# Half feature tiles as pairs of 64-row score matmuls, one projection ahead of the scores, and a last store issued before its waits, in a diffusion transformer block

## The chip, the cores and the metric

The kernel runs on one core of one Trainium2 chip. The metric is device time in microseconds (us) for one execution. Three plain runs of the kernel before are given, and one further execution taken with the hardware profiler. "Faster" and "slower" below are against the median of the plain runs.

## The reference

One block of a diffusion transformer, in bfloat16, for 2 batch rows of 256 tokens (512 tokens together) with 1152 features, 2 heads of 576 features and a hidden layer of 4608.

```python
B, N, D = x.shape            # 2, 256, 1152
H = 2
Dh = D // H                  # 576
mod = (_silu(c) @ w_mod).reshape(B, 6, 1, D)
shift_a, scale_a, gate_a, shift_m, scale_m, gate_m = [mod[:, i] for i in range(6)]
h = _layernorm(x, axis=-1) * (1 + scale_a) + shift_a
qkv = (h @ wqkv).reshape(B, N, 3, H, Dh)
q, k, v = (qkv[:, :, 0].copy(), qkv[:, :, 1].copy(), qkv[:, :, 2].copy())
attn = _softmax(jnp.einsum('bqhd,bkhd->bhqk', q, k) * Dh ** (-0.5), axis=-1)
a = jnp.einsum('bhqk,bkhd->bqhd', attn, v).reshape(B, N, D) @ wo
x = x + gate_a * a
h2 = _layernorm(x, axis=-1) * (1 + scale_m) + shift_m
m = _gelu(h2 @ w_fc1) @ w_fc2
return x + gate_m * m
```

## The kernel before

The 1152 features are nine tiles of 128, so a head of 576 features is four and a half tiles. Feature tiles stand on the 128 partitions, tokens along the free axis. `QK` holds 18 tiles of 512 tokens: Q tiles 0 to 8 and K tiles 9 to 17. Head 0 has Q tiles 0 to 3 and the lower half (partitions 0 to 63) of tile 4; head 1 has the upper half of tile 4 and tiles 5 to 8. K tile 13 is shared by the heads in the same way.

The program is first recorded as units (a unit is one instruction on most engines, or a group of matmuls on TensorE) with the regions of memory that they read and write, and from these `Sched` derives which must wait for which. TensorE (PE) and the queue of SyncE (SP) run in the order in which the code writes them. VectorE (DVE), ScalarE (ACT) and GpSimd (POOL) have a written order for their first instructions (`S.first`) and after that the order of a small cost model: of the units that are ready, the one with the longest path behind it. `emit` then writes the engines' streams, with semaphore waits ahead of the instructions that need them.

The stages on PE, in the order written:

1. Modulation, layer norm transposes and the K projection, paced by the first weights to land.
2. The Q projection of tiles 0 to 5, one feature tile of the input at a time, into six PSUM banks (`qb`). Then `qk_evac` copies each bank to `QK`, on ACT and DVE in turn (`ev_rr`). Tile 4 is an exception: ACT copies its lower half to `QK[0:64, 4]`, whose upper half a memset (`z4a`, in `S.first` of DVE) has set to zero, and DVE copies its upper half to `Q4B`, whose lower half is zero. So each head has its own 128-row form of the shared tile, with zeros in the other head's rows.
3. Q tiles 6, 7 and 8 (`proj`, nine matmuls of 512 columns each) and the scores, in turns. `s_and_softmax(b, h)` computes the scores of one batch row and head in one bank (`s_bank`): for each of two query tiles (`jq`) five accumulating matmuls of 256 columns (`head_chunks`; -1 stands for `Q4B`), so 40 in all. Behind each block DVE finds the row maxima (L934) and scales them, ACT takes the exponential (L938), and DVE normalises (L942).
4. The V projection (`v_proj`), with the transposes of the four probability blocks (`pt_transposes`) between its pieces, and `rows`, which computes the remaining modulation rows with four column-tiled matmuls side by side (`quad_mm`).
5. Attention times V (`pv`), the output projection (`wo_tile`) with the second layer norm, fc1 with GELU, and fc2.

The output leaves in fc2: for each of four token tiles pieces of the 1152 features, in the last tile of widths 384, 384, 224, 96 and 64. Of each piece DVE multiplies by the gate (L1145) and adds the residual (L1146), and SP stores it. These are 14 stores. In `run_engine` SP waits, ahead of the last store, for the landing of all stores but the last two:

```python
if ins is last_out:
    for o in outs[:-2]:
        eng_handle.wait_ge(dma_sems[o.dma_sem], o.dma_val)
```

and after it for the last two. All DMA issues are recorded at L662, all ordinary matmuls at L681, the copies out of PSUM at L676 (ACT) and L678 (DVE).

Of the kernel before, what the change touches and what calls it, by code (L numbers as in the profile page):

```python
# [171 lines left out]
class Sched:  # L172
# [225 lines left out]
    def emit(self, nc, block, sems, dma_sems):  # L398
        order = self.order
        eidx = {e: 0 for e in ENGINES}  # L400
        dma_cnt = [0] * len(dma_sems)
        n_other = getattr(self, "n_other_dma_sems", 8)
        n_sp = len(dma_sems) - n_other
        di = 0
        dj = 0
        for e in ENGINES:
            for u in order[e]:
                for ins in u.instrs:
                    if u.dma_bytes > 0:
                        if e == "sp":  # L410
                            k = di % n_sp
                            di += 1
                        else:
                            k = n_sp + dj % n_other
                            dj += 1
                        dma_cnt[k] += 16
                        ins.dma_sem = k
                        ins.dma_val = dma_cnt[k]
                    else:
                        eidx[e] += 1  # L420
                        ins.eidx = eidx[e]
        self.final_counts = dict(eidx)
        self.final_dma = list(dma_cnt)
        snap = {}
        stats = {"waits": 0}

        def sem_of(d):
            if d.dma_sem is not None:
                return ("d", d.dma_sem), d.dma_val
            return ("e", d.unit.eng), d.eidx  # L430

        allu = sorted(self.units, key=lambda u: (u.start, u.uid))
        known = {e: {} for e in ENGINES}
        waits = {}
        for u in allu:
            e = u.eng
            kn = known[e]
            for ins in u.instrs:
                need = {}
                for d in ins.deps:  # L440
                    k, v = sem_of(d)
                    if need.get(k, 0) < v:
                        need[k] = v
                wl = []
                for k, v in sorted(need.items(), key=lambda kv: (-kv[1], str(kv[0]))):
                    if kn.get(k, 0) >= v:
                        continue
                    wl.append((k, v))
                    kn[k] = v
                    for d in ins.deps:  # L450
                        if sem_of(d) == (k, v):
                            sn = snap.get(d.gidx)
                            if sn:
                                for kk, vv in sn.items():
                                    if kn.get(kk, 0) < vv:
                                        kn[kk] = vv
                            break
                waits[ins.gidx] = wl
                stats["waits"] += len(wl)
                snap[ins.gidx] = dict(kn)  # L460
        self.wait_stats = stats

        outs = [ins for u in order["sp"] for ins in u.instrs if ins.is_out]
        last_out = outs[-1]

        def run_engine(e, eng_handle):
            for u in order[e]:
                for ins in u.instrs:
                    if ins is last_out:
                        for o in outs[:-2]:  # L470
                            eng_handle.wait_ge(dma_sems[o.dma_sem], o.dma_val)
                    for (k, v) in waits[ins.gidx]:
                        if k[0] == "d":
                            eng_handle.wait_ge(dma_sems[k[1]], v)
                        else:
                            eng_handle.wait_ge(sems[k[1]], v)
                    bi = ins.fn(eng_handle)
                    if ins.dma_sem is not None:
                        bi.then_inc(dma_sems[ins.dma_sem], 16)
                    else:  # L480
                        bi.then_inc(sems[e], 1)
            if e == "sp":
                for o in outs[-2:-1]:
                    eng_handle.wait_ge(dma_sems[o.dma_sem], o.dma_val)
                eng_handle.wait_ge(dma_sems[last_out.dma_sem], last_out.dma_val)

        block.sync(lambda eng: run_engine("sp", eng))
        block.tensor(lambda eng: run_engine("pe", eng))
        block.scalar(lambda eng: run_engine("act", eng))
        block.vector(lambda eng: run_engine("dve", eng))  # L490
        block.gpsimd(lambda eng: run_engine("pool", eng))
# [25 lines left out]
def c_mm(n):  # L517
    return max(n / 2.4 + 2.5, 27.0)
# [26 lines left out]
def build_kernel(nc, x, c, wqkv, wo, w_mod, w_fc1, w_fc2, out):  # L545
    S = Sched()
# [4 lines left out]
    with (  # L551
# [11 lines left out]
        def ps32(bank, c0=0, n=512):  # L563
            return psum[:, bank * 512 + c0: bank * 512 + c0 + n]
# [100 lines left out]
        def dve(cost, fn, reads, writes, name):  # L665
            return S.op("dve", cost, fn, reads=reads, writes=writes, name=name)
# [192 lines left out]
                k_pair((KT - 2, KT - 1), i, b)  # L859

        def qk_evac(j, bank):
            if j == 4:
                for eng, dst, src in (("act", QK[0:64, 4, :], psum[0:64, bank * 512:bank * 512 + 512]),
                                      ("dve", Q4B[64:128, :], psum[64:128, bank * 512:bank * 512 + 512])):
                    copy_on(eng, dst, src, 512, False, "qk_ev4" + eng)
                return
            copy_on("act" if ev_rr[0] % 2 == 0 else "dve", QK[:, j, :], ps32(bank), 512, False, "qk_ev%d" % j)
            ev_rr[0] += 1

        def proj(W, j, dst_j, H, bank):  # L870
# [1 line left out]
            for kt in range(KT):  # L872
                mm(ps32(bank), W[:, kt, j * 128:(j + 1) * 128], H[:, kt, :], kt == 0, kt == KT - 1)
            qk_evac(dst_j, bank)

        dve(330, lambda e: e.memset(QK[64:128, 4, :], 0.0), [], [QK[64:128, 4, :]], "z4a")

        def quads(w, g0, g1, q):
            return w.rearrange("p (g q c) -> p g q c", q=4, c=32)[:, g0:g1, q, :]
# [16 lines left out]
        for kt in range(KT):  # L896
            for b in range(2):
# [5 lines left out]
                else:  # L903
# [6 lines left out]
        S.first = {  # L910
# [5 lines left out]
        }  # L916


        head_chunks = {0: [(0, 9), (1, 10), (2, 11), (3, 12), (4, 13)], 1: [(-1, 13), (5, 14), (6, 15), (7, 16), (8, 17)]}
        s_bank = {(0, 0): 4, (1, 0): 5, (0, 1): 6, (1, 1): 3}  # L920

        def s_and_softmax(b, h):
            idx = b * 2 + h
            bank = s_bank[(b, h)]
            S.unit("pe", 10 * c_mm(256), "S_%d_%d" % (b, h))
            ch = head_chunks[h]
            for jq in range(2):
                for ci, (gq, gk) in enumerate(ch):
                    q0 = b * 256 + jq * 128
                    l = Q4B[:, q0:q0 + 128] if gq < 0 else QK[:, gq, q0:q0 + 128]  # L930
                    mm(ps32(bank, jq * 256, 256), l, QK[:, gk, b * 256:(b + 1) * 256], ci == 0, ci == len(ch) - 1)
            s3 = ps32(bank).rearrange("p (j k) -> p j k", j=2)
            mx, nb, rsum, ri, pp = MX[:, idx, :], NB[:, idx, :], RS[:, idx, :], RI[:, idx, :], PP[idx]
            dve(c_dve_psum32(512), lambda e: e.tensor_reduce(out=mx, in_=s3, axis=AX.X, op=ALU.max), [s3], [mx], "smax_%d" % idx)  # L934
            dve(165, lambda e: e.tensor_scalar(out=nb, in0=mx, scalar1=-SCALE, scalar2=None, op0=ALU.mult), [mx], [nb], "snb_%d" % idx)
            for jq in range(2):
                o, i_, bb, aa = pp[:, jq, :], ps32(bank, jq * 256, 256), nb[:, jq:jq + 1], rsum[:, jq:jq + 1]
                act(c_act(256, 1) + 200, lambda e, o=o, i_=i_, bb=bb, aa=aa: e.activation(out=o, in_=i_, func=ACTF.Exp, scale=SCALE, bias=bb, accum_out=aa),  # L938
                    [i_, bb], [o, aa], "sexp_%d_%d" % (idx, jq))
            dve(165, lambda e: e.reciprocal(out=ri, in_=rsum), [rsum], [ri], "sri_%d" % idx)  # L940
            rib = ri.unsqueeze(2).broadcast_to([P, 2, 256])
            dve(c_dve_tt16(512), lambda e: e.tensor_tensor(out=pp, in0=pp, in1=rib, op=ALU.mult), [pp, ri], [pp], "spn_%d" % idx)  # L942
# [131 lines left out]
        for j in range(KG):  # L1074
            qk_evac(j, qb[j])
        proj(WQ, 6, 6, HX, 0)
        s_and_softmax(0, 0)
        proj(WQ, 7, 7, HX, 1)
        s_and_softmax(1, 0)
        proj(WQ, 8, 8, HX, 2)  # L1080
        v_proj(0, 0)
        s_and_softmax(0, 1)
        v_proj(0, 1)
# [119 lines left out]
```

## Time and profile before

| | us |
|---|---|
| median of the three plain runs | 248.95 |
| lowest and highest of the three | 248.63 and 249.59 |
| the profiled execution, its own time | 249.1 |
| span of the profiled execution, first to last instruction | 247.1 |
| PE busy, matmuls | 240.4 |
| PE busy, weight loads (they overlap the matmuls) | 148.0 |
| DVE busy | 69.9 |
| ACT busy | 64.0 |
| POOL busy | 21.1 |

Times inside a view are in us from the start of the span. The profiled execution takes 2.0 us more than its span; the sums of the prediction are made against that execution. "PEld" is the weight load of a matmul, "SPq" the queue on which SyncE issues DMAs, and `<-` ahead of a name in brackets tells whom an engine waited for. A matmul's recorded duration includes its way through the array: successive matmuls overlap, so the cost of one is the distance between starts, not the duration. A few matmul records are missing from the trace. In the view of stretches the columns are the stretch, its length, the busy time of PE, PEld, DVE, ACT and POOL with the number of instructions, the granted share of PE's clock, the busy share of the 16 DMA engines, and GB/s. In the view of DMA issues the columns are the transfer, the queue, the count, KB each and the us from issue to landing.

### The profile page before, as it was taken

Reading aid. Unit: us, or ns where it says so; the run is one execution under the profiler, and the core shown is the slowest. Engines: PE = TensorE matmul, PEld = TensorE weight load, DVE = VectorE, ACT = ScalarE, POOL = GpSimd, SP = SyncE. Lnnn points to the kernel's source line nnn. Section 1 sums busy time; section 2 is a strip of 40 time slices with the busy share of each in tenths; the row PEclk is TensorE's granted clock in tenths of the full one; section 3 lists DMA queues with packets and bytes.
Section 4 is the critical chain, followed back from the end, with each engine's and each line's share of the span. In section 5 each row is a group of like instructions: output and inputs, shape, how many; then the busy total and the mean of one; then the engine's idle time right before and its main releaser. Section 6 shows DMA issues by size and latency. Waiting matters only on the chain.

```text
span 247.1 us, 4020 instructions
## 1 busy us (share of the span) xinstructions
PE 240.4 (97%) x1757; PEld 148.0 (60%) x1767; DVE 69.9 (28%) x179; ACT 64.0 (26%) x130; POOL 21.1 (9%) x35
## 2 busy tenths in 40 slices
PE   7999999999999999999999999999999999999993
PEld 2589844566656766798544444444666666666683
DVE  3742440546222779850000000000022111111122
ACT  5630340344312306983323332223000000000000
POOL 1300000000034175600000000000000000000000
PEclk9999999999999999999999999999999999999998
DMA  7999999999999999999953450000000000000000
GB/s 242 360 376 392 391 369 412 422 428 423 400 382 323 327 369 391 390 376 397 352 159 102 170 191 0 0 3 0 0 19 16 16 16 30 20 16 19 16 16 20
DMA packets 27708, 51.59 MB, mean 209 GB/s; under 512 B 1563, under 2 KB 15659, under 8 KB 26539
## 3 DMA queue, kind: packets, MB, share of 16 engines
q1 hardware_dynamic: 27216, 50.14, 56.1%
q0 software_dynamic: 448, 1.19, 1.5%
q8 instruction: 14, 0.23, 0.4%
q14 instruction: 3, 0.02, 0.0%
q10 hardware_dynamic: 27, 0.00, 0.0%
HBM read 50.14 MB, written 1.19 MB: 208 GB/s over the span
## 4 chain that ended last, share of the span: by engine, by line
PE 92%; DMA 3%; ACT 1%; SPq 1%; issue 0%; DVE 0%
PE psum L681 91%; DMA arena<-in_w_mod_dram 3%; PE psum L684 2%; ACT arena L1056 1%; SPq L662 1%; ACT arena L1040 1%; DVE arena L786 0%; DVE arena L1145 0%; DVE arena L1146 0%; DVE arena L777 0%
## 5 line engine op out<-in xcount | busy, mean ns | idle before, releaser
L681 PE MATMUL psum<-arena 128*128 128x384 bf16 (+8 forms) x1668 | 237.0, 312 | 2.4 <-POOL arena L704 1.4
L681 PEld LDWEIGHTS psum<-arena 128*128 128x128 bf16 (+1 forms) x1678 | 142.5, 97 | 92.2 <-issue 3.6
L1145 DVE TENSOR_TENSOR arena<-psum,arena 128x384 f32<-128x384 f32 (+3 forms) x14 | 7.0, 500 | 119.2 <-PE psum L681 119.2
L1066 ACT ACTIVATE arena<-psum 128x512 bf16<-128x512 f32 (+1 forms) x44 | 22.5, 522 | 42.6 <-PE psum L681 42.6
L676 ACT ACTIVATE arena<-psum 128x512 bf16<-128x512 f32 (+7 forms) x30 | 15.7, 546 | 35.7 <-PE psum L681 33.3
L678 DVE CAST arena<-psum 128x512 bf16<-128x512 f32 (+3 forms) x21 | 13.0, 627 | 26.4 <-PE psum L681 26.3
L1035 POOL TENSOR_TENSOR arena<-arena 128x384 f32<-128x384 f32 x12 | 10.9, 911 | 10.5 <-DVE arena L1034 9.3
L725 DVE BATCH_NORM_STATS2 arena<-arena 128x6 f32<-128x384 f32 (+1 forms) x18 | 9.5, 549 | 1.1 <-DMA arena<-in_x_dram 1.0
L1040 ACT ACTIVATE arena<-arena 128x1152 bf16<-128x1152 f32 x4 | 5.4, 1352 | 9.5 <-DVE arena L1039 9.5
L662 POOL DMA_DIRECT2D dit_scratch<-arena x4 | 2.7, 669 | 60.3 <-ACT arena L676 60.3
L684 PEld LDWEIGHTS psum<-arena 128*128 128x128 bf16 (+1 forms) x89 | 5.9, 98 | 2.7 <-DMA arena<-in_c_dram 0.8
L684 PE MATMUL psum<-arena 128*128 128x128 bf16 (+1 forms) x89 | 7.3, 219 | 0.2
L1034 DVE TENSOR_TENSOR arena<-psum,arena 128x384 f32<-128x384 f32 x12 | 6.6, 548 | 3.2 <-PE psum L681 2.6
L1146 DVE TENSOR_TENSOR arena<-arena 128x384 bf16<-128x384 f32 (+3 forms) x14 | 7.0, 501 | 0.5
L1056 ACT ACTIVATE arena<-psum,arena 128x128 bf16<-128x128 bf16 x16 | 6.1, 460 | 3.2 <-PE psum L684 2.5
L1053 DVE TENSOR_SCALAR arena<-psum,arena 128x128 bf16<-128x128 bf16 x20 | 5.5, 336 | 2.0 <-PE psum L684 1.8
L938 ACT ACTIVATE arena<-psum,arena 128x256 bf16<-128x256 f32 x8 | 3.7, 470 | 6.9 <-PE psum L681 5.4
L729 POOL TENSOR_TENSOR arena<-arena 128x1 f32<-128x1 f32 x6 | 3.3, 551 | 8.3 <-DVE arena L728 8.3
L901 ACT ACTIVATE arena<-arena 128x256 bf16<-128x256 bf16 x6 | 2.5, 495 | 3.3 <-DVE arena L895 3.3
L934 DVE TENSOR_REDUCE arena<-psum 128x2 f32<-128x512 f32 x4 | 2.8, 690 | 1.5 <-PE psum L681 1.5
L786 DVE TENSOR_SCALAR arena<-psum,arena 128x256 bf16<-128x256 bf16 x7 | 2.4, 349 | 2.7 <-PE psum L684 1.4
L942 DVE TENSOR_TENSOR arena<-arena 128x512 bf16<-128x512 bf16 x4 | 2.7, 687 | 0.1
(37 smaller groups left out, 32.0 us busy)
## 6 DMA issues: line engine op xcount, KB each, us to landing
arena<-in_w_mod_dram SPq DMA_DIRECT2D x3, 3456.0 KB, 26.5
arena<-in_w_fc_dram SPq DMA_DIRECT2D x9, 1152.0 KB, 8.8
arena<-in_w_fc_dram SPq DMA_DIRECT2D x4, 2592.0 KB, 20.9
arena<-in_wqkv_dram SPq DMA_DIRECT2D x18, 288.0 KB, 10.0
arena<-in_w_mod_dram SPq DMA_DIRECT2D x3, 864.0 KB, 12.5
arena<-in_wqkv_dram SPq DMA_DIRECT2D x1, 2592.0 KB, 10.9
arena<-in_wo_dram SPq DMA_DIRECT2D x1, 2592.0 KB, 39.0
arena<-in_w_mod_dram SPq DMA_DIRECT2D x3, 480.0 KB, 7.3
```

Of the source, the lines that this page charges most:

```text
L676: act(c_act(n), lambda e: e.activation(out=dst, in_=src, func=ACTF.Copy), [src], [dst], name)
L678: dve(c_dve_psum16(n) if psum16 else c_dve_psum32(n), lambda e: e.tensor_copy(dst, src), [src], [dst], name)
L681: S.instr(lambda e: e.matmul(o, lhsT=l, rhs=r, start=st, stop=sp, **kw), reads=[l, r], writes=[o])
L684: S.instr(lambda e: e.transpose(o, i_, idn), reads=[i_, idn], writes=[o])
L725: dve(550, lambda e, s=s, o=o: e.bn_stats(out=o, in_=s), [s], [o], "bn_%s_%d" % (tag, ci))
L1034: dve(550, lambda e, o=o, ga=ga, x1c=x1c: e.tensor_tensor(out=x1c, in0=o, in1=ga, op=ALU.mult), [o, ga], [x1c], "wo_t1_%d_%d" % (t, ci))
L1035: S.op("pool", 930, lambda e, xs=xs, x1c=x1c: e.tensor_tensor(out=x1c, in0=x1c, in1=xs, op=ALU.add), reads=[x1c, xs], writes=[x1c], name=" ...
L1040: act(1344, lambda e: e.activation(out=xn2, in_=x1, func=ACTF.Identity, scale=rs, bias=nm), [x1, rs, nm], [xn2], "xn2_%d" % t)
L1056: act(440, lambda e, o=o, dst=dst, s1=s1, s2=s2: e.activation(out=dst, in_=o, func=ACTF.Identity, scale=s1, bias=s2), [o, s1, s2], [dst], ...
L1066: act(c_act(ntok), lambda e: e.activation(out=dst, in_=o, func=ACTF.Gelu_apprx_tanh), [o], [dst], "gelu_%d_%d" % (f, tok0))
L1145: dve(c_dve_psum32(w), lambda e, o=o, gm=gm, t1=t1: e.tensor_tensor(out=t1, in0=o, in1=gm, op=ALU.mult), [o, gm], [t1], "fc2_t1_%d_%d" % ( ...
L1146: dve(c_dve_32(w), lambda e, t1=t1, x1c=x1c, ost=ost: e.tensor_tensor(out=ost, in0=t1, in1=x1c, op=ALU.add), [t1, x1c], [ost], "fc2_out_%d ...
```

## The change

Three things change.

- The scores. `qk_evac` copies Q tile 4 whole, like any other tile; the zeroed halves, the memset `z4a` and the use of `Q4B` in the scores go. A new unit, `s_halves`, computes the part of the scores that comes from the half tiles, for all four blocks at once: eight matmuls that each use 64 rows, for head 0 rows 0 to 63 and for head 1 rows 64 to 127 (`tile_position=(64 * h, 0)`), the two heads next to each other in the order. They open the accumulation in the blocks' banks. The blocks themselves then add four full tiles, eight matmuls instead of ten.
- The order on PE. Q tile 7 is projected right after Q tile 6, then come `s_halves`, the first score block, Q tile 8 and the second score block.
- The last store. SP no longer waits ahead of its issue for earlier stores; all waits for stores stand after it.

As tile 4 no longer has a copy of its own on both engines, Q tiles 4 to 8 are now copied by DVE, ACT, DVE, ACT, DVE. `Q4B` is still set to zero at the start, since the warm-up matmuls read it.

```diff
         def run_engine(e, eng_handle):
...
-                    if ins is last_out:
-                        for o in outs[:-2]:
-                            eng_handle.wait_ge(dma_sems[o.dma_sem], o.dma_val)
                     for (k, v) in waits[ins.gidx]:
...
             if e == "sp":
-                for o in outs[-2:-1]:
+                for o in outs[:-1]:
                     eng_handle.wait_ge(dma_sems[o.dma_sem], o.dma_val)
                 eng_handle.wait_ge(dma_sems[last_out.dma_sem], last_out.dma_val)
...
         def qk_evac(j, bank):
-            if j == 4:
-                for eng, dst, src in (("act", QK[0:64, 4, :], psum[0:64, bank * 512:bank * 512 + 512]),
-                                      ("dve", Q4B[64:128, :], psum[64:128, bank * 512:bank * 512 + 512])):
-                    copy_on(eng, dst, src, 512, False, "qk_ev4" + eng)
-                return
             copy_on("act" if ev_rr[0] % 2 == 0 else "dve", QK[:, j, :], ps32(bank), 512, False, "qk_ev%d" % j)
...
-        dve(330, lambda e: e.memset(QK[64:128, 4, :], 0.0), [], [QK[64:128, 4, :]], "z4a")
...
-        head_chunks = {0: [(0, 9), (1, 10), (2, 11), (3, 12), (4, 13)], 1: [(-1, 13), (5, 14), (6, 15), (7, 16), (8, 17)]}
+        head_chunks = {0: [(0, 9), (1, 10), (2, 11), (3, 12)], 1: [(5, 14), (6, 15), (7, 16), (8, 17)]}
         s_bank = {(0, 0): 4, (1, 0): 5, (0, 1): 6, (1, 1): 3}
+
+        def s_halves():
+            S.unit("pe", 4 * c_mm(256) + 100.0, "S_halves")
+            for b in range(2):
+                for jq in range(2):
+                    for h in range(2):
+                        r = slice(64 * h, 64 * h + 64)
+                        q0 = b * 256 + jq * 128
+                        mm(ps32(s_bank[(b, h)], jq * 256, 256), QK[r, 4, q0:q0 + 128], QK[r, 13, b * 256:(b + 1) * 256],
+                           jq == 0, False, skip_group_check=True, tile_position=(64 * h, 0))
 
         def s_and_softmax(b, h):
...
-                    l = Q4B[:, q0:q0 + 128] if gq < 0 else QK[:, gq, q0:q0 + 128]
-                    mm(ps32(bank, jq * 256, 256), l, QK[:, gk, b * 256:(b + 1) * 256], ci == 0, ci == len(ch) - 1)
+                    mm(ps32(bank, jq * 256, 256), QK[:, gq, q0:q0 + 128], QK[:, gk, b * 256:(b + 1) * 256], False, ci == len(ch) - 1,
+                       skip_group_check=True)
...
         proj(WQ, 6, 6, HX, 0)
+        proj(WQ, 7, 7, HX, 1)
+        s_halves()
         s_and_softmax(0, 0)
-        proj(WQ, 7, 7, HX, 1)
+        proj(WQ, 8, 8, HX, 2)
         s_and_softmax(1, 0)
-        proj(WQ, 8, 8, HX, 2)
         v_proj(0, 0)
```

More of the change, by code (lines that the diff above doesn't have):

```diff
@@ L924, in s_and_softmax @@
             bank = s_bank[(b, h)]
-            S.unit("pe", 10 * c_mm(256), "S_%d_%d" % (b, h))
+            S.unit("pe", 8 * c_mm(256), "S_%d_%d" % (b, h))
             ch = head_chunks[h]
```

2 rows, old and new, of the table s2 are left out of this document.

## The prediction

> **What bounds the kernel now.** I began with the page: busy shares, granted clock and the chain that ended last.
>
> ```profile
> PE 240.4 (97%) x1757; PEld 148.0 (60%) x1767; DVE 69.9 (28%) x179; ACT 64.0 (26%) x130; POOL 21.1 (9%) x35
> ...
> PEclk9999999999999999999999999999999999999998
> ...
> PE 92%; DMA 3%; ACT 1%; SPq 1%; issue 0%; DVE 0%
> ```
>
> PE is the bound, at full clock. From the Q projection at 31.5 us to the last matmul at 243.2 us PE shows one wait for another engine, 0.3 us at 99.5 us for ACT's L1056. So PE time removed from the scores counts in full, and VectorE or ScalarE work removed counts for nothing unless PE waits for it. The chain's last compute piece ends at 243.75 us, but the span is 247.1 us: 3.35 us at the end hold no compute. The waits of the DMA queue's own engine, the end of the timeline and the DMA issues after 241 us say what does:
>
> ```profile
> SPq L471 <- DMA out_dram<-arena: 1.9, 1, 1.9
> SPq L485 <- DMA out_dram<-arena: 1.1, 1, 1.1
> ```
>
> ```profile
> 243.52 0.23 DVE L1146 TENSOR_TENSOR arena<-arena 128x64 bf16<-128x64 f32 x1
> ...
> 245.28 0.33 SPq L662 DMA_DIRECT2D out_dram<-arena  x1
> ```
>
> ```profile
> q8 instruction: 1, 0.02, 1.7%
> ...
> out_dram<-arena SPq DMA_DIRECT2D x1, 56.0 KB, 3.8
> out_dram<-arena SPq DMA_DIRECT2D x1, 24.0 KB, 2.7
> out_dram<-arena SPq DMA_DIRECT2D x1, 16.0 KB, 1.4
> ```
>
> The last store's data is ready at 243.75 us and the store is issued at 245.28: SP stands at L471 for the 56 KB store, which was issued at 241.35 and lands at 245.14. The usual 96 KB store lands in 1.6 us. The trace's packets say why this one is late: a 16 KB instruction fetch (queue q8) holds one of the 16 DMA engines from 242.47 for 1.6 us, and that engine writes its eight packets of the 56 KB store only from 244.07, then its eight of the 24 KB store until 244.65. The stretches of the DMA show it: about one engine of 16 busy (0.08), long after the others had finished.
>
> ```profile
> 243.75:244.05 0.30, 0.00 (x0) 0.00 (x0) 0.00 (x0) 0.00 (x0) 0.00 (x0) 1.00 0.00 0
> 244.07:244.67 0.60, 0.00 (x0) 0.00 (x0) 0.00 (x0) 0.00 (x0) 0.00 (x0) 1.00 0.08 9
> ```
>
> Then the stage that the change rewrites: matmuls by shape from 44.9 to 66 us, one score block and the column-tiled `rows` block as stretches, and the weight loads around `rows`.
>
> ```profile
> L681 PE MATMUL psum<-arena 128*128 128x256 bf16 x40 | 5.0, 273 | 0.0
> ...
> 46.84:47.93 1.09, 1.09 (x11) 0.98 (x10) 0.84 (x2) 0.60 (x1) 0.00 (x0) 1.00 0.97 405
> ...
> 66.31:70.81 4.49, 4.49 (x109) 2.48 (x109) 0.00 (x0) 0.49 (x1) 0.00 (x0) 1.00 1.05 392
> ```
>
> ```profile
> 66.31 4.16 PEld L681 LDWEIGHTS psum<-arena 128*2 128x2 bf16 x108 [0.32 <-issue]
> 70.80 0.28 PEld L681 LDWEIGHTS psum<-arena 128*128 128x128 bf16 x3 [0.33 <-issue]
> ```
>
> Ten score matmuls start over 1.09 us: 0.109 us each, 40 of them 4.37 us. A full-height weight load lasts 98 ns but goes ahead under the matmul before it.
>
> **The change, part by part.**
>
> *Scores.* Eight matmuls per block remain (32 in all), and the halves of tile 4 and tile 13 become eight 64-row matmuls in four pairs, put ahead of all four blocks. Removed: 8 x 0.109 = 0.87 us (the two heads each spent two 128-row matmuls per batch row on the shared tiles, half of the rows zero). Added: four pairs. No row shows two row tiles side by side. The nearest is `rows`: four column-tiled matmuls of 384 columns start 2 to 4 ns apart, and the next four 163 ns later, the price of one. By that a pair costs 0.11 us, four 0.44 us. The far end is one after the other, 0.87 us. I take 0.44, since each pair uses different rows, operands and banks (4 with 6, 5 with 3).
>
> Going into the column-tiled block costs more: 256 ns between starts at 66.06 and 66.31 where 163 is usual (+93), and 268 ns from the last group's first start to the next full matmul at 70.81 (+105). The idle of 0.32 and 0.33 us ahead of the loads above is the same: the array's loads no longer go ahead. So one visit costs 0.20 us. It is bounded by zero, if row tiles need no change of the array, and by these 0.20. I take 0.20, the only measured case. The Trainium skill (TensorEngine Tiling (Array Packing), Key Properties) says that a change of tiling mode drains TensorE; this trace agrees with about 0.1 us each way, for column tiles.
>
> Scores: -0.87 + 0.44 + 0.20 = **-0.23 us**; ends -0.44 (free visit) and +0.20 (no overlap).
>
> The Trainium skill (TensorE: Matmul & The Clock Gate, LDWEIGHTS (loading the stationary operand)) gives a load of 128 columns as 128 / 1.2 GHz, 107 ns, whatever its rows; by it alone the two loads of a pair would take an estimated 213 ns, and the scores would come to +0.18 us. The trace disagrees for full-height loads: the 2-column matmuls at 10.8 us, each with a 128-column load of its own, start 26 ns apart, so two loads fit under one score matmul.
>
> *Order and evacuations.* Q tile 7 now runs right after tile 6, into bank 1, which ScalarE must have emptied of Q tile 5. ScalarE's copies start at 45.10, 45.59 and about 46.09 and last 0.60 us: free at 46.69, and PE gets there at 46.84. The cover is 0.15 us; without it PE would lose what ScalarE is late by. Tile 4's evacuation becomes one copy instead of two half copies (0.69 us on VectorE, third in its queue, done at about 47.0; the halves run at 48.8). The 64-partition memset z4a goes: VectorE, under the K matmuls, nothing. The first score block ends 2.4 us later than before, at 50.3 us (a projection of 1.94 us and the pairs' 0.64 come ahead of it, two matmuls of its own go); before, its softmax was through 3.6 us after the block, and its transposes are due at 59.5 us, so 5 us are left. The last block ends at about 57.7 us as before; its transposes are due at 64.3. The number of instructions on PE is the same, 1767 matmuls. No SP or POOL queue is passed by what moves: no DMA moves with tile 7. Sum: 0.
>
> *Does the scores' gain reach the end?* The weights that PE uses after 60 us land well ahead (the first fc1 weights at 78.1 us, used after 99), and the ScalarE wait at 99.5 us hangs on PE's own transposes. I count it in full.
>
> *Last store.* Its waits move behind its issue. VectorE ends at 243.75 and SP issues 27 ns later, as for the other stores: 243.77, 1.51 us earlier. What is late next is the slow DMA engine: its packets of the last store queue behind those of the 24 KB store, which lands at 245.30 whatever SP does. The 56 and 24 KB stores land 0.16 us apart; one more such step gives 245.46. From the last landing to the end the trace has 247.10 - 246.69 = 0.41 us, and one more wait pair now stands behind it (the five at L471 stand 60 to 75 ns apart): 0.47. End: 245.93, **-1.17 us**. Best: landing with the 24 KB store, 245.30 + 0.41 = 245.71, -1.39. Worst: landing as slowly as the 56 KB store, 3.79 us: 247.56 + 0.47 = 248.03, +0.93. I take the middle one because the engine that decides is named by the packets. Nobody waits behind SP's later waits: nothing is queued there but the end.
>
> *Sum.* -0.23 - 1.17 = -1.40 us on the profiled execution's 249.1 us (span 247.1 and 2.0 around it): 247.7. The median of 248.95 lies 0.15 below that execution, so I forecast **247.55 us**. About 0.5%, 1.25 us, is what a measurement of this kernel can tell from no change; the three runs spread over 0.96.
>
> **The rivals.**
>
> *The pairs don't pay (0.15).* If a pair's members run one after the other, or if the next pair's loads wait for the array's rows, the scores cost +0.20 instead of -0.23: 248.0 us. For it: no row tile in the trace, and each pair loads 2 x 128 columns where `rows` loads 2 a tile. Against it: the column tiles' perfect overlap. The Trainium skill (TensorE: Matmul & The Clock Gate, Measured speedup vs the span model) has four row tiles 3.07 times as fast as one by one; no run here shows it.
>
> *The end was not what it seemed (0.11).* The 1.5 us at L471 exist only when the instruction fetch falls into the 56 KB store. In the ordinary 1.6 us that store lands at 242.95, before the data of the last one is ready, and the waits moved cost nothing where they are. Then only the scores' -0.23 is left: 248.7 us. For it: fetches come on PE's schedule, and the profile is one execution. Against it: the profiled 249.1 agrees with the plain median to 0.15 us, and PE's instruction count, which places the fetch, is unchanged.
>
> *The last store becomes the straggler (0.08).* Issued into the jam, the 128-byte packets may fare as the 448-byte ones did: landing after 3.79 us gives 248.03 and, less the scores' 0.23, +0.70: 249.65 us, slower. It decides from a landing of 3.1 us on (1.41 before); from 4.3 us on it is slower by over 0.5%. For it: the two stores in flight then, and the jam. Against: the fetch ends at 244.09, before the packets of a store issued at 243.77 would start (0.83 us after issue in the trace).
>
> Something unforeseen, either sign: 0.06.
>
> **How the numbers follow.** The forecast case has 0.60; it spans -1.0 to -1.83 us, and of it 0.54 is beyond 1.25 us, since the unknown sizes lean to the better ends and the fetch-bound landing is an upper one. Faster by over 0.5%: 0.54 and 0.02 unforeseen, 0.56. Within: 0.06 of the forecast, 0.15, 0.11 and 0.04 of the third rival, 0.36. Slower: 0.04 and 0.04 unforeseen, 0.08. The range goes from both best ends, 248.95 - 1.83 = 247.1, past the second rival's 248.7 to 248.8; what it leaves out is the third rival, part of the unforeseen and edges.
>
> **What would show it.** After: the last store issued 0.03 us after VectorE's last L1146, no wait ahead of it, 1.5 to 1.7 us from issue to landing, about 2.2 us from the last compute to the end of the span (3.35 before). In the scores: members of a pair starting a few ns apart, pairs 0.11 us apart, about 0.1 us of extra spacing before and after, PE's last matmul 0.2 us earlier. I am wrong if pair members start 0.1 us apart, if PE waits in front of Q tile 7, or if the 16 KB store lands over 2 us after its issue.

## The result, and the profile after

The changed kernel takes 247.22 us (median; 247.05 to 247.37, 4 runs), the kernel before in the same comparison 249.0 us (248.63 to 249.59, 4 runs). The ratio is 0.9932 (95% interval 0.9907 to 0.9956): 1.78 us less, where 1.40 had been forecast. The profiled execution took 247.28 us with a span of 245.30; before it was 249.1 and 247.13.

The busy shares of the changed kernel, as on its page: PE is as much the bound as before.

```profile
PE 241.0 (98%) x1767; PEld 147.4 (60%) x1767; DVE 69.3 (28%) x178; ACT 63.3 (26%) x129; POOL 21.1 (9%) x35
```

Then the end of the changed kernel in four views: what SP waited for, VectorE's last instruction, the last store, and the DMA issues after 240.7 us (KB, us to landing). Line numbers are shifted in this kernel: L659 issues DMAs, L678 is the matmul, L1146 and L1147 are the two VectorE steps of fc2; L481 and L482 are the waits after the last issue.

```profile
SPq L482 <- DMA out_dram<-arena: 0.4, 1, 0.4
SPq L481 <- DMA out_dram<-arena: 0.2, 1, 0.2
```

```profile
243.18 0.23 DVE L1147 TENSOR_TENSOR arena<-arena 128x64 bf16<-128x64 f32 x1
...
243.44 0.33 SPq L659 DMA_DIRECT2D out_dram<-arena  x1
```

```profile
out_dram<-arena SPq DMA_DIRECT2D x1, 56.0 KB, 3.2
out_dram<-arena SPq DMA_DIRECT2D x1, 24.0 KB, 2.1
out_dram<-arena SPq DMA_DIRECT2D x1, 16.0 KB, 1.4
```

The 1.9 us in which SP stood ahead of the last store are gone. The store is issued 0.03 us after its data (1.53 before) and lands after 1.41 us as before, at 244.84; what SP waits for behind it overlaps the landing. From the last compute to the end of the span it is 1.89 us (245.30 - 243.41), where it was 3.39.

The scores: matmuls by shape from 44.8 to 66 us, and the weight loads around the pairs.

```profile
L678 PE MATMUL psum<-arena 128*128 128x256 bf16 x32 | 4.2, 273 | 0.0
...
L678 PE MATMUL psum<-arena 64*128 64x256 bf16 x8 | 0.6, 272 | 0.0
```

```profile
48.76 0.33 PEld L678 LDWEIGHTS psum<-arena 64*128 64x128 bf16 x8 [0.42 <-issue]
49.31 0.22 PEld L678 LDWEIGHTS psum<-arena 128*128 128x128 bf16 x3 [0.21 <-issue]
```

Forty matmuls became 32 and eight half-height ones, and the eight take 0.55 us from the first load to the next full one, the way out included. By the starts in the trace, members of a pair begin 4 ns apart and pairs 0.11 us apart; the last full matmul ahead of them begins 0.31 us earlier where 0.216 is usual (+0.095), and from the last pair to the next full matmul it is 0.205 where 0.109 is usual (+0.096). The first pair and the first full matmul take 11 ns more each.

To see what this is worth without the noise of the start I use one stretch in all traces below, called PE's stretch: from the first matmul on the third piece of modulation weights (10.79 us in the chain before, 10.69 after) to the start of the last matmul. Before it is 232.05 us (to 242.85), after 231.82 us (to 242.51). So of the 1.84 us between the two spans 0.23 are the scores, 1.50 the end, and 0.11 only the moment at which the third piece of the first weights landed.

### The profile page after: what moved, and what is told of

It is laid out like the page before. It is cut to its first block, busy times and chain, and to the rows that moved or that the text cites. A ratio compares the mean times of both kernels' runs of the same rounds, so it can differ in the third digit from the quotient of the medians.

```text
span 245.3 us, 4026 instructions
## 1 busy us (share of the span) xinstructions
PE 241.0 (98%) x1767; PEld 147.4 (60%) x1767; DVE 69.3 (28%) x178; ACT 63.3 (26%) x129; POOL 21.1 (9%) x35
## 4 chain that ended last, share of the span: by engine, by line
PE 93%; DMA 3%; ACT 1%; SPq 1%; DVE 0%; issue 0%
PE psum L678 91%; DMA arena<-in_w_mod_dram 3%; PE psum L681 2%; ACT arena L1056 1%; SPq L659 1%; ACT arena L1040 1%; DVE arena L783 0%; DVE arena L1146 0%; DVE arena L1147 0%; DVE arena L774 0%
## 5 line engine op out<-in xcount | busy, mean ns | idle before, releaser
L678 PE MATMUL psum<-arena 128*128 128x384 bf16 (+8 forms) x1678 | 237.7, 312 | 1.6 <-POOL arena L701 1.4
L678 PEld LDWEIGHTS psum<-arena 128*128 128x128 bf16 (+1 forms) x1678 | 142.0, 97 | 92.8 <-issue 4.7
L1146 DVE TENSOR_TENSOR arena<-psum,arena 128x384 f32<-128x384 f32 (+3 forms) x14 | 7.0, 500 | 119.2 <-PE psum L678 119.2
L673 ACT ACTIVATE arena<-psum 128x512 bf16<-128x512 f32 (+6 forms) x29 | 15.1, 545 | 40.9 <-PE psum L678 39.0
L675 DVE CAST arena<-psum 128x512 bf16<-128x512 f32 (+2 forms) x21 | 13.0, 627 | 26.3 <-PE psum L678 26.2
L659 POOL DMA_DIRECT2D dit_scratch<-arena x4 | 2.7, 669 | 60.1 <-ACT arena L673 60.1
L1147 DVE TENSOR_TENSOR arena<-arena 128x384 bf16<-128x384 f32 (+3 forms) x14 | 7.0, 501 | 0.5
```

Source lines behind the costliest of these rows:

```text
L673: act(c_act(n), lambda e: e.activation(out=dst, in_=src, func=ACTF.Copy), [src], [dst], name)
L675: dve(c_dve_psum16(n) if psum16 else c_dve_psum32(n), lambda e: e.tensor_copy(dst, src), [src], [dst], name)
L678: S.instr(lambda e: e.matmul(o, lhsT=l, rhs=r, start=st, stop=sp, **kw), reads=[l, r], writes=[o])
L1146: dve(c_dve_psum32(w), lambda e, o=o, gm=gm, t1=t1: e.tensor_tensor(out=t1, in0=o, in1=gm, op=ALU.mult), [o, gm], [t1], "fc2_t1_%d_%d" % ( ...
L1147: dve(c_dve_32(w), lambda e, t1=t1, x1c=x1c, ost=ost: e.tensor_tensor(out=ost, in0=t1, in1=x1c, op=ALU.add), [t1, x1c], [ost], "fc2_out_%d ...
```

## The experiments

Theory: PE gains 0.23 us in the scores, the last store 1.2 to 1.5 us at the end, and the latter exists because an instruction fetch holds one DMA engine and with it the 56 KB store. Rivals: one part brings all; the fetch is innocent; the pairs are cheap for another reason.

**One part at a time.** First the store alone in the kernel before:

```diff
-                    if ins is last_out:
-                        for o in outs[:-2]:
-                            eng_handle.wait_ge(dma_sems[o.dma_sem], o.dma_val)
...
-                for o in outs[-2:-1]:
+                for o in outs[:-1]:
```

> The kernel before with one part of the change: the waits for earlier stores stand behind the issue of the last store; scores and order as before. Theory: most of the 1.78 us comes from here. The last store is issued 0.03 us after VectorE's last instruction instead of 1.5 us after it, from the last compute to the end of the span it takes 1.9 to 2.2 us instead of 3.4, and the time falls by 1.2 to 1.5 us (to about 247.6). Rival (the wait was hidden anyway, or the last landing is set by the other stores): from the last compute to the end still over 3 us, time within 0.3 us of before.

Measured: 247.62 us against 248.53, ratio 0.9963 (0.995 to 0.9975), so 0.91 us and less than the 1.2 expected. PE's stretch is 232.05 us as before; the last store goes out 0.03 us after its data, and it is 1.90 us from the last compute to the end.

Then the scores alone: the changed kernel with these same lines put back.

> The changed kernel with the waits put back ahead of the last store, as before; scores in pairs and Q tile 7 ahead. Theory: PE's stretch from the end of Q tile 6 to the first V projection is 0.23 us shorter over the scores' whole stage, the end keeps its 3.4 us after the last compute as long as an instruction fetch holds back the 56 KB store: time 0.2 to 0.3 us below before. Rival (the scores bring most of it): more than 1 us below before.

Measured: 248.50 us against 248.53, ratio 0.9997 (0.9985 to 1.0008): plain runs cannot tell it from no change, and the interval still holds a gain of 0.23 us. The trace tells it: PE's stretch is 231.82 us, 0.23 less, and SP stands again ahead of the last store. Its waits:

```profile
SPq L471 <- DMA out_dram<-arena: 1.4, 1, 1.4
SPq L485 <- DMA out_dram<-arena: 1.1, 1, 1.1
```

Here the fetch held its engine for 1.27 us instead of 1.61, the 56 KB store landed after 3.27 us instead of 3.79, and the end took 2.87 us instead of 3.39. So the end with the waits ahead is no constant.

**Is it the fetch?** The kernel before and the changed one, each with PE's stream 142 instructions longer at the start, so that the fetch comes earlier against the stores:

```diff
+        for i in range(76):
+            S.unit("pe", 27.0, "pad_%d" % i)
+            mm(ps32(2, 0, 2), Q4B[:, 0:128], Q4B[:, 0:2], True, True)
...
-        warm(15, "b")
+        warm(10, "b")
```

> The kernel before, with 76 two-column matmuls on zeros put at the very start of PE's stream and five of the fifteen 512-column warm-ups left out, so that PE's stream is 142 instructions longer and its last instruction fetch comes some 3 us earlier against the stores. Theory (the fetch holds one DMA engine and with it the 56 KB store): the 56 KB store lands in 1.6 to 2.0 us instead of 3.8, the wait ahead of the last store is over before its data is ready, and the end falls from 3.4 to about 1.9 us behind the last compute although the waits stand where they stood: about 1.5 us less, less what the start may cost. Rival (448-byte rows are slow by themselves, or the waits cost by themselves): landing stays near 3.8 us and the end near 3.4 us.

> The changed kernel with the same addition at the start of PE's stream. Theory: the last store lands 1.41 us after its issue already with the fetch where it is, so nothing is left to gain: the end stays at about 1.9 us behind the last compute, the same as in the changed kernel to 0.1 us, and the difference to the kernel before with the same addition is the scores' 0.23 us alone. Rival (part of the end is still the fetch): over 0.2 us less behind the last compute than in the changed kernel.

The last DMA issues of the kernel before with this addition:

```profile
out_dram<-arena SPq DMA_DIRECT2D x1, 56.0 KB, 1.9
out_dram<-arena SPq DMA_DIRECT2D x1, 24.0 KB, 1.5
out_dram<-arena SPq DMA_DIRECT2D x1, 16.0 KB, 1.4
```

The last fetch now starts at 236.6 us, 7.7 us ahead of the last compute instead of 1.3. The 56 KB store lands after 1.85 us, and the end is 1.95 us with the waits still ahead of the last store; the store's issue comes 0.09 us after its data instead of 0.03, which is all that the waits cost by themselves. In the changed kernel the end stays 1.90 us. So the fetch is shown to hold back the 56 KB store, and the rival, that 448-byte rows are slow by themselves, falls.

In time the first of the two missed: 248.24 us, 0.9986 (0.9977 to 0.9996), where about 1.5 us less was expected; the changed kernel with the addition has 248.26 us, 0.9984 (0.9975 to 0.9994), about what the kernel before with it has, so the scores' 0.23 us cannot be seen between them (PE's stretch tells them apart: 232.07 and 231.82 us). The two traces show a late start: PE begins its stretch at 11.39 and 11.88 us, in the traces without the addition at 10.69 to 11.30. So a part of what was gained at the end was given back at the start, and not for the same reason in both. In the kernel before with the addition the third piece of weights lands at 11.02 us, as in other traces (10.64 to 11.26), but PE is not ready for it: its 512-column warm-up matmuls still start 0.427 us apart up to 8.6 us, where in the trace before they start 0.216 us apart from 6.6 us on, and the transposes behind them start 0.107 us apart until 9.3 us, instead of 0.056. Why is open. In the changed kernel with the addition PE is in time and the third piece is late, at 11.83 us. The addition has also moved the first fetch from 16 us to 7.5 and 8.5 us, in between the first weights; whether that fetch or something else made the third piece late was not tried.

**Do pairs run side by side?** The order within the eight is changed so that neighbours use the same rows:

```diff
-            for b in range(2):
-                for jq in range(2):
-                    for h in range(2):
+            for h in range(2):
+                for b in range(2):
+                    for jq in range(2):
```

> The changed kernel with the eight 64-row matmuls in another order: the four of head 0 first, then the four of head 1, so that neighbours use the same rows of the array. Theory (the pairs run side by side, and only neighbours on different rows can): starts 0.109 us apart throughout, the stage 0.33 to 0.44 us longer than in the changed kernel, one overlap being left where the heads meet. Rival (64-row matmuls are cheap by themselves): spacing unchanged, stage as in the changed kernel.

The theory as I had put it falls. 247.51 us, 0.9959 (0.9946 to 0.9972), and the stage is unchanged, here in the weight loads:

```profile
49.66 0.34 PEld L678 LDWEIGHTS psum<-arena 64*128 64x128 bf16 x8 [0.42 <-issue]
50.22 0.33 PEld L678 LDWEIGHTS psum<-arena 128*128 128x128 bf16 x4 [0.21 <-issue]
```

0.56 us instead of 0.55. (PE's stretch is 0.36 us longer, but that arises at 19.8 us, in the K projection, where PE waits for a piece of modulation weights, and not here.) The starts still come in twos, now 14 ns apart: 49.668 and 49.682, 49.788 and 49.802, and so on. If matmuls on the same rows take 0.109 us each, one after the other, no two of one head can begin so close together, and the fifth matmul of the program begins before the second. Whether that is so, or half-height matmuls are simply cheap, the next one tells: the four of head 1 are left out.

```diff
-                    for h in range(2):
+                    for h in range(1):
...
-                    mm(ps32(bank, jq * 256, 256), QK[:, gq, q0:q0 + 128], QK[:, gk, b * 256:(b + 1) * 256], False, ci == len(ch) - 1,
+                    mm(ps32(bank, jq * 256, 256), QK[:, gq, q0:q0 + 128], QK[:, gk, b * 256:(b + 1) * 256], h == 1 and jq == 0 and ci == 0, ci == len(ch) - 1,
```

> The changed kernel with the four half-tile matmuls of head 1 left out, so that head 1's scores lack the half tile; four 64-row matmuls on the same rows remain. Theory (the two heads' matmuls run side by side): the stretch from Q tile 7 to the first full score matmul is as long as with all eight, 0.855 us from start to start, to 0.03 us. Rival (64-row matmuls cost half of a full one, one after the other): 0.2 us shorter.

```profile
49.38 0.33 PEld L678 LDWEIGHTS psum<-arena 64*128 64x128 bf16 x4 [0.42 <-issue]
49.92 0.33 PEld L678 LDWEIGHTS psum<-arena 128*128 128x128 bf16 x4 [0.21 <-issue]
```

Four take 0.54 us, eight 0.55; from start to start 0.851 us against 0.855. The four start 0.11 to 0.12 us apart, so half-height matmuls on the same rows are not cheap by themselves. PE's stretch is 231.83 us, as with all eight. Head 1's half tiles cost nothing beside head 0's: they run at the same time. (One run, 248.13 us.) This trace holds a find on the fetch as well: PE's stream is eight instructions shorter, the fetch starts 0.75 us ahead of the last compute instead of 1.3, the packets of the 56 KB store are already through, and it is the 24 KB store that is held:

```profile
out_dram<-arena SPq DMA_DIRECT2D x1, 56.0 KB, 1.8
out_dram<-arena SPq DMA_DIRECT2D x1, 24.0 KB, 2.4
out_dram<-arena SPq DMA_DIRECT2D x1, 16.0 KB, 1.7
```

**The price of a visit.** Two pairs ahead of the first block, two ahead of the second:

```diff
-        s_halves()
+        s_halves((0,))
         s_and_softmax(0, 0)
         proj(WQ, 8, 8, HX, 2)
+        s_halves((1,))
         s_and_softmax(1, 0)
```

> The changed kernel with the half tiles in two visits of two pairs, one ahead of the first score block and one ahead of the second, instead of one visit of four pairs. Theory (each change of the array's tiling costs about 0.1 us each way): PE 0.2 us longer than in the changed kernel, which uses up nearly all that the pairs bring. Rival (the extra spacing at the first pair is a wait of another kind, for a copy or a semaphore): no change.

247.77 us, 0.9969 (0.9959 to 0.998). PE's stretch is 232.07 us, 0.25 longer than in the changed kernel and no better than before. Each of the two visits shows the same gaps in the loads, 0.42 and 0.21 us:

```profile
48.81 0.12 PEld L678 LDWEIGHTS psum<-arena 64*128 64x128 bf16 x4 [0.42 <-issue]
49.14 2.50 PEld L678 LDWEIGHTS psum<-arena 128*128 128x128 bf16 x17 [0.21 <-issue]
52.06 0.11 PEld L678 LDWEIGHTS psum<-arena 64*128 64x128 bf16 x4 [0.42 <-issue]
52.39 0.66 PEld L678 LDWEIGHTS psum<-arena 128*128 128x128 bf16 x7 [0.21 <-issue]
```

The first waits on VectorE's semaphore, the second on none, and their gaps are equal, so it is no wait for a copy.

**The order of tile 7.** Tiles 7 and 8 back in their old places behind the score blocks, the pairs right after tile 6.

```diff
-        proj(WQ, 7, 7, HX, 1)
         s_halves()
         s_and_softmax(0, 0)
-        proj(WQ, 8, 8, HX, 2)
+        proj(WQ, 7, 7, HX, 1)
         s_and_softmax(1, 0)
+        proj(WQ, 8, 8, HX, 2)
```

> The changed kernel with Q tiles 7 and 8 in their old places, behind the first and the second score block, so that the half-tile matmuls follow Q tile 6. Theory: VectorE's copy of Q tile 4 is done only at about 47.0 us while PE gets there at about 46.8, so PE waits 0.15 to 0.25 us ahead of the first pair, and the order of tile 7 is worth that much. Rival (the wait and the change of tiling overlap, so the wait is hidden): PE no later than in the changed kernel to 0.05 us.

247.50 us, 0.9957 (0.9942 to 0.9972), and PE's stretch is 231.83 us, as in the changed kernel. PE is no later, as the rival said, but not for its reason: there is no wait to hide. I had taken the copies to run in the order of the tiles. The scheduler does not: in this kernel and in the changed one VectorE copies tile 2, then 4, then 0, so tile 4 is done at 46.4 us, before PE gets there at 46.9.

**How large is it usually?** The changed kernel and the kernel before once more, unchanged, and the changed one waiting at the end for the last three stores only (`for o in outs[-3:-1]` instead of `outs[:-1]`).

> The changed kernel once more, to set it beside the two half changes. The store alone gave 0.91 us and the scores alone 0.03 us in plain runs (interval -0.2 to 0.4). Theory (the parts add up, the scores bring 0.23 us on PE as in every trace, and the 1.5 us of the first profile's end are more than the usual): 1.0 to 1.3 us below before. Rival (the two together are worth more than their sum, as the first comparison's 1.78 us says): 1.6 us or more.

> The kernel before, profiled once more. Theory (the end's length is set by where and for how long the instruction fetch holds one DMA engine): the 56 KB store lands between 3.2 and 3.8 us after its issue, following the fetch's duration (1.0 to 1.6 us), and from the last compute to the end it takes 2.8 to 3.4 us. Rival (the first profile's 3.4 us is fixed): 3.39 us to 0.05.

> The changed kernel, waiting at the end for the last three stores only (the earlier ones have long landed by then, and VectorE's reuse of their buffers waits for most of them). Theory: the wait pair behind the last landing goes, from the last landing to the end 0.39 us instead of 0.45; time 0.06 us less, which plain runs can't tell from the changed kernel. Rival (the waits are taken one by one after the last landing): 0.2 us less or more.

The changed kernel: 248.07 us against 249.22, 0.9956 (0.994 to 0.9973), 1.15 us less. That is near the sum of the parts: 0.91 from the store alone in plain runs and 0.23 from the scores by the traces. Its stretch is 231.82 us and its end 1.90 us. The kernel before: its waits are

```profile
SPq L471 <- DMA out_dram<-arena: 1.6, 1, 1.6
SPq L485 <- DMA out_dram<-arena: 1.1, 1, 1.1
```

with a fetch of 1.44 us, a landing of the 56 KB store after 3.46 us and an end of 3.06 us; stretch 232.05 us. What sets the end can be read from all traces that have the fetch near it, by when the fetch ends, counted from the end of the last compute (plus is later, all times in us):

| trace | waits | fetch ends | last store, issue to landing | last compute to end |
|---|---|---|---|---|
| before | ahead | +0.34 | 1.41 | 3.39 |
| before again | ahead | +0.01 | 1.42 | 3.06 |
| scores alone | ahead | -0.18 | 1.42 | 2.87 |
| changed | behind | -0.27 | 1.41 | 1.89 |
| two visits | behind | -0.23 | 1.41 | 1.89 |
| store alone | behind | -0.10 | 1.41 | 1.90 |
| changed again | behind | -0.05 | 1.42 | 1.90 |
| tile 7 in place | behind | -0.01 | 1.43 | 1.91 |
| waiting for three stores | behind | +0.08 | 1.52 | 2.00 |
| heads one after the other | behind | +0.19 | 1.62 | 2.10 |
| one head's half tiles | behind | +0.21 | 1.65 | 2.13 |

With the waits ahead the end comes 3.05 us after the fetch has ended, three times out of three. With the waits behind the end comes 1.89 to 1.90 us after the last compute when the fetch ends 0.05 us or more ahead of that, and 1.91 to 1.92 us after the fetch's end when the fetch ends with it or later. So the change takes the fetch out of the end only where the fetch is over in time.

Waiting for three stores only: 247.31 us, 0.9933 (0.991 to 0.9957). That is 0.76 us below the changed kernel in the same comparison, but the trace gives no reason for it in the waits: from the last landing to the end 0.46 us (0.45 in the changed kernel, 0.39 expected), stretch 231.84 us, end 2.00 us. The two profiles differ in when the stretch starts, 10.69 against 11.05 us, which the changed waits at the end cannot cause. A wait and a branch still follow the landing. So the expected 0.06 us are not there, and whether this kernel is faster than the changed one, which had 247.22 us in the first comparison, is open.

## Why the prediction was right

The time of 247.22 us lies in the range, 0.33 below the forecast and 0.1 above its lower edge, and the forecast case came in: scores and end both gain. The forecast of 1.40 us lies between the two comparisons of the changed kernel, 1.78 and 1.15 us.

- **Scores, -0.23 us forecast, -0.23 measured** in every trace with one visit of four pairs, but for the one that lost 0.36 us to late weights elsewhere. Pair price 0.11 (0.109 to 0.110) and visit price 0.20 (0.095 + 0.096, and 11 ns twice) were both taken from the column-tiled `rows` block, and both held for row tiles. The Trainium skill (TensorEngine Tiling (Array Packing), Key Properties) says that a change of tiling mode drains TensorE; the extra 0.095 and 0.096 us agree with that. The Trainium skill's 107 ns for a load of 128 columns (TensorE: Matmul & The Clock Gate, LDWEIGHTS (loading the stationary operand)) would have made two loads, one after the other, the bound of a pair. In the trace a load of a pair lasts 0.093 to 0.096 us, near that figure, but the two loads of a pair start 4 ns apart, so they run side by side and the pairs start 0.109 us apart.
- **End, -1.17 us forecast, -1.50 measured** between the two profiles. The wait and what was behind it were right; the term for the last landing was mis-sized, and its reason was not the one I gave. The last store was to queue behind the packets of the 24 KB store on the slow engine and land at 245.46 in before's time, 1.69 us after its issue; it landed after 1.41. In the changed kernel the fetch lasted 1.05 us instead of 1.61 and ended 0.30 us ahead of the last issue, and the store met nothing. Where the fetch ended 0.06 to 0.19 us after the issue (three rows of the table) the last store was late, but not as I had it: all its 128 packets start late, 0.93 to 1.07 us after the issue instead of 0.83, when the slow engine has been through with the 24 KB store for 0.3 to 0.7 us, and it lands 1.46 to 1.47 us after the end of the fetch. Why all of them are held is open. With before's fetch, which ended at 244.09, that gives an estimated landing at 245.55 and a gain of 1.13 us, so my 245.46 was near by luck, and the rest of the 1.50 is where the fetch fell in the second profile. And the added wait pair cost about 0.01 us, not 0.06: 0.44 us from the last landing to the end before (to 247.13, which the page rounds), 0.45 after.
- **Order and copies, 0 forecast, 0 measured**, but the cover of 0.15 us that I named was misread: ScalarE copies tile 5 first, not third, so bank 1 was free over a microsecond before PE came. The sum did not hang on it: even the third of ScalarE's copies ends at 46.56 us, 0.17 us before PE starts tile 7 at 46.73.
- **The rivals.** The pairs pay. The last store did not become the straggler; its landing took 1.41 to 1.43 us in ten of the thirteen traces and 1.65 at most. But the argument against that rival, that a fetch which ends before the store's packets would start does no harm, fails in the three late ones. The second rival, that the end was not what it seemed, is half true: the 3.39 us of the first profile was the longest of three, and the store alone gave 0.91 us in plain runs, not 1.17.
- **The amount.** 1.78 us in one comparison and 1.15 in another are not told apart by a cause, and their intervals overlap. The kernel before has medians of 249.0, 248.53, 248.52 and 249.22 us in four comparisons, the last of them on another chip than the two ahead of it. Across the eleven profiles without the addition at the start, the start of PE's stretch, set by the landing of the third piece of weights, moves between 10.69 and 11.30 us. The stretch itself is 232.05 to 232.07 us in the four traces with the old scores and 231.82 to 231.84 in seven of the eight with the half tiles in one visit; the eighth is the one with 0.36 us lost at 19.8 us. Why the first weights land at different times is open.

## What to carry to other kernels

A wait for old work ahead of the last issue is free only as long as nothing delays that work; put it behind the issue, where the landing hides it. Read the end from several profiles before pricing it: here it was 2.87 to 3.39 us with the waits ahead. A change of the array's tiling had the same price at each visit, about 0.21 us, so gather all small matmuls of one tiling into one visit: here four pairs saved 0.44 us and one visit took 0.21 of it, and with two visits nothing was left. And read the scheduler's order before naming the cover of a copy.

## What the runs showed of the hardware

- The trace before has 14 instruction fetches of 16 KB for about 3,530 instructions of PE (1767 matmuls, each with a load), one in about 250. The last one moves with the length of PE's stream: 7.7 us instead of 1.3 ahead of the last compute with 142 instructions more, 0.75 us with eight fewer. A fetch lasts 0.9 to 1.6 us, and eight of the 128 packets of a store under way, the share of one engine in 16, come only after it: the 56 KB store then lands after 3.2 to 3.8 us, and after 1.7 to 1.9 with no fetch beside it. A shift of eight instructions moved the harm from the 56 KB store to the 24 KB one.
- A store issued up to 0.19 us ahead of the fetch's end landed 1.46 to 1.47 us after that end, instead of 1.41 us after its issue.
- Matmuls on different row tiles ran as two streams: with four of head 0 ahead of four of head 1 in the program, they still started in twos, 14 ns apart, where four of one head alone start 0.11 to 0.12 us apart. Neighbourhood in the program was not needed within these eight.
- A visit of row tiles cost about what the visit of column tiles did: 0.095 us in and 0.096 out here, 0.093 and 0.105 there.
